# Wider r-u-k sums, one MLP step moved to an earlier slot, and weight sums spread over four slots

## The chip, the cores and the metric

The kernel runs on one core of one Trainium2 chip. The metric is the device time of one execution in microseconds (us); lower is better. TensorE does the matrix products, VectorE and GpSimd the elementwise work, ScalarE copies and activations; nearly all loads and stores go through one queue (q1 moved 54.88 of the 56.65 MB in the kernel before), issued one after another by SyncE; ScalarE issues five loads. Every timed run also has the mean clock granted to TensorE, as a share of full speed.

## The reference

Linear attention with a decay per step (RWKV-6), then a LayerNorm and an MLP with ReLU, all in fp32. Sizes: 4 batches, 8 heads, 768 steps, head width 48, model width 384, hidden width 1536.

```python
for t in range(S):
    cur = np.einsum('bhd,bhe->bhde', u[None] * kt, vt)
    y[:, :, t] = np.einsum('bhd,bhde->bhe', rt, state + cur)
    state = wt[:, :, :, None] * state + np.einsum('bhd,bhe->bhde', kt, vt)
# x: y as (B, S, 384)
xn = (x - mu) / np.sqrt(var + 1e-06) * g_ln
out = x + np.maximum(xn @ w_ch1, 0.0) @ w_ch2
```

The term with u needs, for each step and head, the sum over d of r, u and k: the "r-u-k sums".

## The kernel before

The sequence is cut into eight rounds of 384 steps (a batch and a half of the sequence each), a round into two units of four heads. Inside a round, six levels combine ever longer pieces; each level is one *slot*: TensorE forms level products (`a_ps`), VectorE multiplies r and k by decays (`rkT`) and keeps part of the products (`A`). The MLP of an earlier round is cut into steps of a few products (an h or o step is three products of 128x384, each two instructions in the profile, of 323 ns at full clock), and `fill` runs steps between the other tasks of a slot until `UNTIL[slot]` steps are done in all. So `UNTIL` says where in time the MLP's work lies. Rounds are counted from 0 and slots from the first of round 1, so slot 12 is the first of round 3.

```python
UNTIL = [3, 6, 8, 11, 14, 16, 19, 21, 24]
while len(UNTIL) <= 2 * NLEV + NLEV - 2:
    UNTIL.append(UNTIL[-1] + 3)             # slots 12 to 16: 36, 39, 42, 45, 48
while len(UNTIL) < NR * NLEV:
    UNTIL.append(UNTIL[-1] + MLP_STEPS / NLEV)
...
def fill(until, tasks):
    n = int(until + 0.01) - done
    m = max(n, len(tasks))
    for i in range(m):
        for t in tasks[i * len(tasks) // m : (i + 1) * len(tasks) // m]:
            t()
        for _ in range((i + 1) * n // m - i * n // m):
            mlp_step()
```

The r-u-k sums of the first four units are products with a selector that has two columns, one for each head of a pair:

```python
def product_sums(q):
    ...
    for pr in pairs:
        for c in range(TT):
            PE.matmul(ps[:, ts(pr * TT + c, 2)], a["ruk"][pr][:, ts(c, P)],
                      sel[:, NP * g + pr], start=True, stop=True)
```

From round 2 on the second MLP product is done with fewer multiplications (seven products in place of eight), for which VectorE forms four sums of weights once, in slots 17 to 19; the fourth is `nat_r<-more,w_sb` and `more<-more,w_sb` in the profile. `warm(n)` runs products on zeros ("idle" in the profile) that keep TensorE busy.

Of the kernel before, what the change touches and what calls it, by code (L numbers as in the profile page):

```python
# [52 lines left out]
def kernel(  # L53
# [19 lines left out]
    P = 128  # L73
    HP = 64
    C = 64
    NH = 4
    NP = NH // 2
    U = H // NH
    TT = 3
    RN = TT * P  # L80
    NHALF = S // RN
    NK = NP * TT
# [123 lines left out]
    sel = const.tile([P, H // 2, 2], F32, name="sel")  # L206
# [27 lines left out]
    for lev in range(NLEV - 1):  # L234
        n = 1 << lev
# [212 lines left out]
    def product_sums(q):  # L448
        b, f, g = units[q]
        a = st[q]  # L450
        ps = ps_t.tile([P, RN], F32, tag="t", name=f"own_ps{q}")
        for pr in pairs:
            for c in range(TT):
                PE.matmul(
                    ps[:, ts(pr * TT + c, 2)], a["ruk"][pr][:, ts(c, P)],
                    sel[:, NP * g + pr], start=True, stop=True,
                )
        o = a["own"] = p4.tile([P, TT, NH], F32, tag="own", name=f"own{q}")
        ACT.copy(
            out=o.rearrange("p c (r j) -> p r c j", j=2),  # L460
            in_=ps[:, 0 : 2 * NK].rearrange("p (r c j) -> p r c j", r=NP, j=2),
        )

    def own_term(q, eng):
# [443 lines left out]
    def mixed(*lists):  # L908
        return [
            t for _, t in sorted(  # L910
                (((i + 0.5) / len(l), t) for l in lists for i, t in enumerate(l)),
                key=lambda at: at[0],
            )
        ]

    def each(f, *ranges):
        calls = [()]
        for r_ in ranges:
            calls = [c + (x,) for c in calls for x in r_]
        return [lambda c=c: f(*c) for c in calls]  # L920
# [43 lines left out]
    for lev in range(1, NLEV):  # L964
        quads(u0, lev)
        quads(u1, lev)
        run(ahead[2 * lev - 2 : 2 * lev] if lev < NLEV - 1 else [])
        if lev in (2, 3, 4):
            begin()
        if lev == 1:  # L970
            product_sums(u0)
        elif lev < NLEV - 1:
            warm(3)
        for which in ("rk",) if lev < NLEV - 1 else "kr":
            for q in (u0, u1):
                grow(q, lev, which)
        keep(0, lev)
# [11 lines left out]
    exchanged(u0)  # L989
    states(u1)  # L990
    product_sums(u1)
    own_term(u1, POOL)
    scratch = st[u0]["rk"]
# [26 lines left out]
    UNTIL = [3, 6, 8, 11, 14, 16, 19, 21, 24]  # L1020
    while len(UNTIL) <= 2 * NLEV + NLEV - 2:
        UNTIL.append(UNTIL[-1] + 3)
    while len(UNTIL) < NR * NLEV:
        UNTIL.append(UNTIL[-1] + MLP_STEPS / NLEV)
    ahead = [t for nm in "wkr" for t in each(turned, units_of(2), nm, pairs)]
    JOINS, BEGINS = (3, 4, 4, 4, 4, 2), (3, 3, 4, 4, 3)
    for rnd in range(1, NR + 1):
# [3 lines left out]
        for lev in range(NLEV):  # L1031
            slot = (rnd - 1) * NLEV + lev
# [20 lines left out]
            tasks, turning = [], []  # L1053
            if rnd == 1:
                if lev < 2:
                    tasks += each(load, new, "kr"[lev], [SPO])
                if lev == 2:
                    SPO.dma_start(
                        out=u_bc,
                        in_=bass.AP(  # L1060
                            tensor=u.tensor, offset=u.offset, ap=[[0, P], [D, H], [1, D]]
                        ),
# [16 lines left out]
            if rnd == 2 and lev == 2:  # L1079
                tasks += each(load_before, new[:1], [k], [0], [SPO]) + each(load_v, new)  # L1080
                tasks += each(load_before, new[:1], [v], [1], [SPO])
            if slot in (17, 18, 19):
                tasks += each(weight_sums, ((3,), (1,), (2, 4))[slot - 17])
            if rnd == 2 and lev in (3, 4):
                tasks += each(own_term, now[lev - 3 :][:1], [POOL])
            if rnd > 2 and lev == 1:
# [24 lines left out]
            if lev == 3 and rnd > 1:  # L1111
                for q in now:
                    load_vx(q)
                if rnd > 2:
# [6 lines left out]
                    tasks = each(norm, [rnd - 1]) + tasks  # L1121
# [17 lines left out]
            if lev == NLEV - 1:  # L1139
# [7 lines left out]
                if now:  # L1147
                    tasks = mixed(
                        tasks,
                        each(ends, now, pairs) + each(finish, [2, 2, 4])  # L1150
                    )
                if rnd == 1:
                    tasks = [join] * JOINS[lev] + tasks + each(totals, [rnd + 1], [POOL])
            if rnd == 1 and lev < NLEV - 1:

                n = (1, 2, 2, 1, 0, 0)[lev] * NP
                tasks += mixed(
                    [begin] * BEGINS[lev], [join] * JOINS[lev], ahead[:n],
                    each(product_sums, now) if lev == 1 else [],
                )  # L1160
                del ahead[:n]
# [35 lines left out]
```

## Time and profile before

| | before |
|---|---|
| median of the first four runs | 560.83 us (559.22 to 561.71) |
| span of the profiled run | 558.1 us |
| TensorE busy | 539.5 us |
| its waits over 1 us for VectorE | 2.08 us at 167, 2.96 us at 250 |
| stretches at half clock | three, 13.6 us in all |

A table of stretches shows where time lies. I cut it into five (the second, like the last at full clock, is left out). Each line has a stretch of the span, its length, busy time and instructions of TensorE, its weight loads, VectorE, ScalarE and GpSimd, then the granted clock, the share of the DMA engines and GB/s. The cuts are at the statistics of rounds 0, 1, 2 and 3. Of the kernel before:

```profile
0.00:46.00 46.00, 43.84 (x1002) 34.81 (x1002) 32.73 (x66) 24.40 (x52) 17.72 (x54) 0.93 0.78 176
...
124.00:195.00 71.00, 66.17 (x1006) 42.54 (x1005) 59.76 (x98) 14.85 (x32) 28.07 (x22) 0.95 0.57 128
195.00:256.00 61.00, 57.35 (x922) 38.00 (x921) 50.40 (x84) 14.87 (x32) 23.60 (x18) 1.00 0.52 114
256.00:558.00 302.00, 297.52 (x3818) 221.59 (x3816) 163.22 (x335) 67.49 (x144) 60.59 (x55) 1.00 0.30 68
```

More than half of the span, from 256 us on, is TensorE back to back at full clock: 297.5 of 302 us. Nothing that only rearranges work has much to gain there. The clock is short of 1.00 in the first and third stretch, and the fourth has TensorE idle for 3.65 us, most of it the one wait at 250.

### The profile page before, as it was taken

To read this page: it belongs to the slowest core of one execution; us is meant where nothing else is said; L and a number is where in the kernel's file an instruction comes from. 1 tells how busy PE (TensorE), PEld (TensorE's weight loads), DVE (VectorE), ACT (ScalarE), POOL (GpSimd) and SP (SyncE) were. 2 spreads that over 40 slices of the span, in tenths; PEclk is the share of its full clock that TensorE was granted. 3 is DMA by queue.
4 is the path that set the end of the run, shared out by engine and by line. 5 is a ranking of instruction groups with operands and counts; after the bars stand their busy time and mean duration, and the time that the engine had idled before them with its cause. 6 is when DMAs were issued, how large, how long until landed. Compare 5 with 4: busy or idle time off the path is not lost.

```text
span 558.1 us, 18693 instructions
## 1 busy us (share of the span) xinstructions
PE 539.5 (97%) x8114; PEld 387.6 (69%) x8114; DVE 372.7 (67%) x720; ACT 169.6 (30%) x363; POOL 136.8 (25%) x157
## 2 busy tenths in 40 slices
PE   9999999999989999979999999999999999999997
PEld 6777665675656665658766895679766885688567
DVE  4888998959978777988576866778593641251022
ACT  3576887501250016201242015301331025202200
POOL 7140010300764019600482018221460000000000
PEclk9899999999997999999999999999999999999999
DMA  9956877255664584345764484547500000000001
GB/s 234 197 129 134 195 216 187 52 108 95 161 153 95 142 161 92 80 109 123 150 137 96 106 171 109 115 106 148 116 5 3 16 29 1 2 16 28 1 0 42
DMA packets 141554, 56.65 MB, mean 102 GB/s; under 512 B 124449, under 2 KB 130721, under 8 KB 141473
## 3 DMA queue, kind: packets, MB, share of 16 engines
q1 hardware_dynamic: 139600, 54.88, 43.5%
q8 instruction: 63, 1.03, 0.8%
q10 hardware_dynamic: 1872, 0.59, 0.4%
q14 instruction: 19, 0.15, 0.1%
HBM read 48.66 MB, written 4.72 MB: 96 GB/s over the span
## 4 chain that ended last, share of the span: by engine, by line
PE 70%; DVE 13%; DMA 5%; ACT 4%; SPq 3%; issue 2%; POOL 2%; DVEq 0%; ACTq 0%; POOLq 0%
PE h_ps L49 22%; PE z_ps L49 8%; PE a_ps L49 8%; PE o_ps L49 6%; PE x_ps L49 6%; PE y_ps L49 4%; PE v_ps L49 4%; PE y L49 4%; DVE rkT L49 4%; DVE w_sb L49 2%; SPq L165 2%; PE kv L49 2%; DMA r_runs<-in_r_dram 1%; DMA nat_r<-in_r_dram 1%; ACT low L49 1%
## 5 line engine op out<-in xcount | busy, mean ns | idle before, releaser
L49 PE MATMUL h_ps<-xT,w_sb 128*128 128x384 f32 x576 | 198.6, 493 | 2.6 <-ACT hs L49 1.0
L49 PEld LDWEIGHTS h_ps<-xT,w_sb 128*128 128x128 f32 x576 | 104.9, 190 | 71.0 <-ACT hs L49 4.8
L49 ACT ACTIVATE hs<-h_ps 128x384 f32<-128x384 f32 x96 | 47.0, 489 | 160.0 <-PE h_ps L49 159.2
L49 DVE TENSOR_TENSOR rkT<-rkT,tot 128x768 f32<-128x768 f32 (+1 forms) x96 | 79.7, 873 | 21.7 <-PE a_ps L49 12.3
L49 PEld LDWEIGHTS a_ps<-rkT 48*64 48x64 f32 x4128 | 66.4, 138 | 21.0 <-issue 11.6
L49 PE MATMUL a_ps<-rkT 48*64 48x32 f32 x4128 | 71.4, 222 | 3.3 <-DVE rkT L49 3.1
L49 PE MATMUL z_ps<-w_sb,hs 128*128 128x384 f32 x144 | 50.4, 495 | 3.0 <-DVE x L49 3.0
L49 PE MATMUL o_ps<-w_sb,hs 128*128 128x384 f32 x144 | 51.6, 506 | 0.1
L49 POOL TENSOR_TENSOR vo<-v,own 128x576 f32<-128x576 f32 x16 | 19.4, 1211 | 89.1 <-DVE own L49 53.0
L49 POOL TENSOR_TENSOR nat_w<-nat_w,nat_r 128x576 f32<-128x576 f32 x10 | 14.9, 1494 | 106.5 <-DMA nat_w<-in_v_dram 88.9
L49 PEld LDWEIGHTS z_ps<-w_sb,hs 128*128 128x128 f32 x144 | 26.3, 190 | 19.0 <-DVE x L49 3.1
L49 DVE SCALAR_TENSOR_TENSOR s<-s,decay,kv 128x48 f32<-128x48 f32 x160 | 29.3, 257 | 15.0 <-PE kv L49 14.9
L49 PEld LDWEIGHTS o_ps<-w_sb,hs 128*128 128x128 f32 x144 | 26.9, 195 | 17.1 <-issue 1.2
L49 DVE COPY_PREDICATED A<-mask,a_ps 128x768 f32<-128x768 int8 x32 | 38.4, 1198 | 0.0
L49 ACT ACTIVATE rstd<-mv,eps 128x3 f32<-128x3 f32 x8 | 2.4, 297 | 116.9 <-DVE mv L49 116.9
L49 DVE TENSOR_TENSOR x<-y,vo 128x288 f32<-128x288 f32 x32 | 13.1, 450 | 32.5 <-PE y L49 32.4
L49 ACT ACTIVATE xT<-xT_ps,g_sb 128x384 f32<-128x384 f32 x24 | 13.3, 580 | 41.8 <-PE xT_ps L49 41.5
L49 DVE TENSOR_TENSOR low<-hs 128x768 f32<-128x768 f32 x12 | 11.5, 962 | 21.5 <-ACT hs L49 21.5
L49 DVE TENSOR_TENSOR rkT<-rkT,wT 128x768 f32<-128x768 f32 x16 | 24.9, 1591 | 0.9 <-PE a_ps L49 0.8
L49 PE MATMUL y_ps<-w_sb,hs 128*128 128x192 f32 x144 | 25.4, 326 | 0.0
L49 PEld LDWEIGHTS y_ps<-w_sb,hs 128*128 128x128 f32 x144 | 23.4, 190 | 0.0
L49 DVE TENSOR_SCALAR w_sb<-w_sb 128x384 f32<-128x384 f32 (+1 forms) x48 | 20.5, 427 | 0.8
(120 smaller groups left out, 767.7 us busy)
## 6 DMA issues: line engine op xcount, KB each, us to landing
raw<-in_moe_w_ch_dram SPq DMA_DIRECT2D x24, 384.0 KB, 4.0
w_runs<-in_w_dram SPq DMA_DIRECT2D x79, 70.0 KB, 2.0
k_runs<-in_k_dram SPq DMA_DIRECT2D x79, 70.0 KB, 2.0
r_runs<-in_r_dram SPq DMA_DIRECT2D x79, 70.0 KB, 2.0
v<-in_v_dram SPq DMA_DIRECT2D x48, 96.0 KB, 3.3
out_dram<-x SPq DMA_DIRECT2D x24, 192.0 KB, 2.5
nat_r<-in_r_dram SPq DMA_DIRECT2D x42, 96.0 KB, 3.2
nat_k<-in_k_dram SPq DMA_DIRECT2D x42, 96.0 KB, 3.3
```

The lines of the kernel that those rows point to most:

```text
L49: return lambda *args, **kw: self.tc.keep_in_program_order(f(*args, **kw))
L165: eng.dma_start(out=t[ds(HP * j + SQ * e, SQ), 0:n], in_=bass.AP(tensor=src.tensor, offset=first + SQ * e, ap=[[NS * D, SQ], [1, n]]),)
```

## The change

The intent is to keep TensorE at full clock and to take waits from it, without changing what is computed: the r-u-k sums stream 64 columns (32 copies of the two) and ScalarE copies two of each 64; slot 12 gets four MLP steps in place of three, which is paid back in slot 16; the fourth weight sum moves from slot 19 to slot 20.

```diff
 PE.matmul(
-    ps[:, ts(pr * TT + c, 2)], a["ruk"][pr][:, ts(c, P)],
-    sel[:, NP * g + pr], start=True, stop=True,
+    ps[:, ts(pr * TT + c, HP)].rearrange("p (n j) -> p n j", j=2),
+    a["ruk"][pr][:, ts(c, P)],
+    sel[:, NP * g + pr][:, None].broadcast_to([P, HP // 2, 2]),
+    start=True, stop=True,
 )
 ...
-    in_=ps[:, 0 : 2 * NK].rearrange("p (r c j) -> p r c j", r=NP, j=2),
+    in_=ps.rearrange("p (r c n) -> p r c n", r=NP, n=HP)[..., 0:2],
 ...
+UNTIL[12:16] = [37, 40, 43, 46]
 ...
-if slot in (17, 18, 19):
-    tasks += each(weight_sums, ((3,), (1,), (2, 4))[slot - 17])
+if 17 <= slot <= 20:
+    tasks += each(weight_sums, [(3, 1, 2, 4)[slot - 17]])
```

## The prediction

> **What bounds the kernel now.** I read, in this order, the page's shares of busy time, its strip of forty slices, the clock in half-microsecond windows around each dip, the timelines of TensorE and VectorE around its long waits, and the chain of waits. First the shares and the clock strip:
>
> ```profile
> PE 539.5 (97%) x8114; PEld 387.6 (69%) x8114; DVE 372.7 (67%) x720; ACT 169.6 (30%) x363; POOL 136.8 (25%) x157
> PEclk9899999999997999999999999999999999999999
> core 0: 558.1 us, clock 0.988
> ```
>
> TensorE is busy 97% of the span, so only three things can shorten the span: fewer idle gaps on it, a higher clock, or less work. The clock strip has two weak places, slices 1 to 2 and slice 12. A mean clock of 0.988 means 0.012 x 558.1 = 6.7 us of full-speed work lost. Half-microsecond windows (busy time, instructions, granted clock, DMA share, GB/s) show three dips at half clock:
>
> ```profile
> 23.00:23.50 0.50, 0.50 (x23) 1.00 0.67 111
> 23.50:24.00 0.50, 0.50 (x5) 0.54 0.94 183
> 26.50:27.00 0.50, 0.50 (x32) 0.55 0.98 286
> 40.50:41.00 0.50, 0.50 (x7) 0.61 0.00 0
> 44.00:44.50 0.50, 0.50 (x40) 0.98 0.00 0
> 166.50:167.00 0.50, 0.00 (x0) 0.90 0.59 152
> 173.50:174.00 0.50, 0.50 (x3) 0.77 0.15 28
> ```
>
> The dips run from 23.5 to 26.9, from 40.6 to 44.0 and from 166.9 to 173.7: 3.4, 3.4 and 6.8 us, 13.6 in all, half of which is the 6.8 lost. Next, TensorE's timeline (start, length) just ahead of the dips and at its only other long wait:
>
> ```profile
> 20.25 1.50 PE L49 MATMUL own_ps<-sel,ruk 128*128 128x2 f32 x12 [0.24 <-ACT wT L49]
> 37.82 1.50 PE L49 MATMUL own_ps<-sel,ruk 128*128 128x2 f32 x12
> 164.24 0.92 PE L49 MATMUL kv<-v,kn 64*64 64x48 f32 x48
> 167.24 1.51 PE L49 MATMUL a_ps<-rkT 48*64 48x32 f32 x48 [2.08 <-DVE rkT L49]
> 169.29 1.50 PE L49 MATMUL a_ps<-rkT 48*64 48x32 f32 x48 [0.54 <-DVE rkT L49]
> 250.24 2.20 PE L49 MATMUL z_ps<-w_sb,hs 128*128 128x384 f32 x6 [2.96 <-DVE x L49]
> ```
>
> Both early dips follow a window holding the r-u-k sums (two columns streamed per weight load). The third follows a TensorE wait of 2.08 us for VectorE. The last line is a 2.96 us wait without a dip. VectorE's timeline ahead of that one:
>
> ```profile
> 234.70 2.05 DVE L49 TENSOR_TENSOR nat_r<-more,w_sb 128x768 f32<-128x768 f32 x1
> 236.68 0.55 DVE L49 TENSOR_TENSOR more<-more,w_sb 128x384 f32<-128x384 f32 x1
> 237.15 2.90 DVE L49 STREAM_TRANSPOSE wT<-w_runs 128x384 f32<-128x384 f32 x4
> 248.29 0.84 DVE L49 STREAM_TRANSPOSE rkT<-r_runs 128x384 f32<-128x384 f32 x1 [1.17 <-DMA r_runs<-in_r_dram]
> 249.85 0.34 DVE L49 TENSOR_TENSOR x<-z_ps,x 128x192 f32<-128x192 f32 x1
> ```
>
> The x add that TensorE waits for stands in VectorE's order behind a transpose that waits for a load of r. In the chain of waits that load was issued late because the k and r loads reuse the buffers that the four wT transposes free, and those stand behind the fourth weight sum (the first two lines).
>
> [...]the three dips lie on one grid of 3.41 us. [...]12 r-u-k instructions of the chain at 66.98 us take 1.24, or 103 ns each, although only two columns stream. [...]the sum of 128x768 took 2.05 us at 234.70 beside GpSimd, the like one at 210.84 took 0.94.
>
> **Part one: 64 columns in the r-u-k sums.** Four calls of six products, each two instructions. A 128x384 instruction takes 1.94/6 = 323 ns, so 64 columns need an estimated 54 ns of streaming, under the 103 ns of the weight load: the six products keep their 1.24 us. Transposes, with 128 columns, take 1.46/12 = 122 ns, so at worst each call grows 0.1 us. The ScalarE copy still moves 12 values per partition. So the direct cost is 0 to 0.3 us in all. What it buys is activity: 12 x 54 = 0.65 us more streaming in a window of 3.41. Counting for each window streaming time weighted by the share of rows used (columns x 0.84 ns), I get 0.38 and 0.57 for the windows before the first two dips. They become 0.57 and 0.76. Windows that did not trip lie at 0.54 and above; but one of the tripped ones was at 0.57, so the measure is crude and the first window is near the edge.
>
> If the dips go: in the first, the r transposes 1.20 against 0.81 for like ones, two filler instructions 1.28 against 0.65, level products 2.08 against 1.53: 1.6 us. In the second, filler 1.58 against 0.65 and about 100 y products that would take half of 1.9: 1.8 us. Both lie on the chain (TensorE to 45.3, then VectorE's statistics that begin the VectorE-bound stretch of weight conversion), and later waits on loads there are on buffers freed by the same engines. Full value 3.4; I count 75%: 2.5 us.
>
> **Part two: a fourth MLP step in round 3's first slot.** No work is added: the order of the built kernel has one o step of three products (2.03 us at full clock) between the last h step and the second kv of that slot, and one fewer before the last level products of round 3. In the trace's clock: h ends at 164.24, the o step runs to 166.3, kv to 167.1, the level products find their first operand ready at 167.24. Of 2.62 us of wait about 0.14 + 1.25 stay, because the second VectorE product still ends at 169.25. Then three o steps from 170.05 at full clock end at 176.1 instead of 178.26. VectorE itself does not move before 178.3: it is back to back from 162.5. Its wT transposes at 175.3 also anchor the load queue, busy issuing from 176.2 to 202, so r lands at 187.7 as before. But VectorE had 1.61 + 1.30 + 0.36 us idle after 178 and 0.71 + 2.22 later. Walking both queues on, the fourth level products start at 194.4 instead of 196.75, the sixth at 202.0 instead of 205.84, and VectorE's r-u-k reduction at 205.7 instead of 208.92. From there GpSimd and the loads follow VectorE, so 3.2 us is kept. If the dip at 166.9 stays for one window (I give it one in three), 1.6 of that goes. Counted: 2.7 us.
>
> **Part three: weight sums over four slots.** The fourth sum leaves its place ahead of the wT transposes (2.05 + 0.55[...]) for one behind the next mask copy. So the transposes, the loads and r's landing come 2.5 us earlier than part two alone makes them. VectorE then does the sum, 1.45 us, where it waited 0.41 + 0.93 + 1.17. Walking the queue: last transpose ends 243.8, x add 244.9, TensorE resumes at 245.0; it stopped at 244.1. Of the 2.96 wait 0.9 is left: 2.0 us. After 262 TensorE idles little over 1 us in total, so what is gained there reaches the end.
>
> **Sum.** 2.5 + 2.7 + 2.0 = 7.2, less 0.4 for the wider products and small new waits: 6.8. From 560.3 this gives 553.5 us.
>
> **Rivals.** (a) The clock does not answer to columns: part one yields nothing, 556. For it speaks that the windows also hold small y, kv and level products; against it, that windows full of those without r-u-k sums kept full clock. (b) The load queue takes the place of the wait: it issues without pause from 176 to 202, so parts of 3.2 us are given back there and the reduction moves by one only; 556 to 557. Against it stand the 3.6 us that VectorE waited for TensorE at 202.4. (c) [...]an earlier stretch shifts a poor window elsewhere[...]: a new dip costs 1.7; 555. (d) All goes well, no dip left: 560.3 - 3.4 - 3.2 - 2.0 = 551.7.
>
> **Range and chances.** The worst mixtures of (a), (b) and (c) give 558, the best 551; run to run the kernel before spreads 2.5 us[...]. So 549.8 to 557.8 eight times in ten. Faster by over 2% needs 549.1, below the best sum: 0.07. Slower by over 2% would need a new stall of 18 us, of which nothing speaks: 0.01. Within 2%: 0.92.
>
> **What would show it.** Right: no half clock near 24 and 41 us; r-u-k groups still about 1.24 us; the level products of round 3's second slot waiting about 1.3 instead of 2.6; o steps after them at 323 ns; the z wait near 245 under 1.2; the fourth weight sum standing between a mask copy and the transposes of k, each of them not waiting over 1 us for its load; a mean clock of 0.995 or more. Wrong: dips at the same places (rival a), long new VectorE waits on r loads near 187 to 205 (b), a dip after 167 (c).

## The result, and the profile after

The changed kernel takes 553.89 us in the median of four runs (552.47 to 555.32), against 560.83 before. The ratio is 0.988, with a 95% interval of 0.9843 to 0.9916. A ratio here is the mean time of one kernel's fast runs over that of the other's in the same rounds, so it is not quite the ratio of the medians. It is clear of 1.

First the shares, the clock strip and the mean clock of the profiled run after the change:

```profile
PE 535.8 (97%) x8114; PEld 384.7 (70%) x8114; DVE 371.4 (67%) x720; ACT 169.6 (31%) x363; POOL 137.2 (25%) x157
PEclk9999999999998999999999999999999999999999
core 0: 551.7 us, clock 0.997
```

TensorE's instructions are as many as before; one weak slice is left in the strip. The first, third and fourth of the same five stretches, cut at the same statistics:

```profile
0.00:44.00 44.00, 40.99 (x1003) 32.83 (x1004) 33.23 (x67) 24.73 (x53) 18.04 (x54) 1.00 0.78 179
...
121.00:192.00 71.00, 67.13 (x1012) 42.80 (x1012) 60.06 (x99) 14.96 (x32) 28.10 (x22) 0.98 0.55 130
192.00:250.00 58.00, 56.25 (x919) 37.52 (x918) 49.07 (x85) 14.86 (x32) 23.68 (x18) 1.00 0.52 121
```

The cuts are rounded; the statistics themselves start at 46.24, 123.69, 194.78 and 256.02 before, and at 43.82, 121.10, 192.09 and 249.63 after. So the first stretch gave 2.4 us, the second and third 0.3 together, the fourth 3.7; the last 302 us did not change. VectorE's statistics of round 1 and its r-u-k reduction, on which the reading of part two rests, before (first two lines) and after:

```profile
123.69 1.46 DVE L49 BATCH_NORM_STATS2 stats<-x 128x6 f32<-128x384 f32 x3
208.92 0.74 DVE L49 TENSOR_REDUCE own<-rk 128x12 f32<-128x576 f32 x1
121.10 1.45 DVE L49 BATCH_NORM_STATS2 stats<-x 128x6 f32<-128x384 f32 x3
204.52 0.74 DVE L49 TENSOR_REDUCE own<-rk 128x12 f32<-128x576 f32 x1
```

Now the places that the prediction named. TensorE's timeline after the change (start, length, what, wait before it):

```profile
20.13 1.55 PE L49 MATMUL own_ps<-sel,ruk 128*128 128x64 f32 x12 [0.24 <-ACT wT L49]
31.83 1.60 PE L49 MATMUL a_ps<-rkT 48*64 48x32 f32 x96 [0.73 <-DVE A L49]
...
161.27 2.10 PE L49 MATMUL o_ps<-w_sb,hs 128*128 128x384 f32 x6
163.29 0.92 PE L49 MATMUL kv<-v,kn 64*64 64x48 f32 x48
165.01 0.90 PE L49 MATMUL a_ps<-rkT 48*64 48x32 f32 x48 [0.80 <-DVE rkT L49]
167.06 1.39 PE L49 MATMUL a_ps<-rkT 48*64 48x32 f32 x48 [1.15 <-DVE rkT L49]
...
243.85 2.20 PE L49 MATMUL z_ps<-w_sb,hs 128*128 128x384 f32 x6 [1.05 <-DVE x L49]
```

The group of sums takes 1.55 us in this line, 1.50 before. The o step stands where TensorE used to wait, and of 2.62 us of wait 1.95 is left, in two gaps. The z wait is 1.05 instead of 2.96. And there is a small new wait, 0.73 us at 31.8, for VectorE. The granted clock in half-microsecond windows (busy, instructions, clock, DMA share, GB/s):

```profile
23.50:24.00 0.50, 0.50 (x6) 1.00 1.03 207
40.50:41.00 0.50, 0.50 (x45) 1.00 0.00 0
...
167.00:167.50 0.50, 0.44 (x22) 0.75 0.70 137
170.50:171.00 0.50, 0.50 (x3) 0.84 0.91 163
```

Both early dips are gone; the third is still there, behind two gaps of 0.80 and 1.15 us, one window (3.4 us) long instead of two. Finally VectorE ahead of the z wait:

```profile
237.27 0.95 DVE L49 TENSOR_TENSOR nat_r<-more,w_sb 128x768 f32<-128x768 f32 x1
238.14 0.55 DVE L49 TENSOR_TENSOR more<-more,w_sb 128x384 f32<-128x384 f32 x1
241.88 0.86 DVE L49 STREAM_TRANSPOSE rkT<-r_runs 128x384 f32<-128x384 f32 x1 [1.06 <-DMA r_runs<-in_r_dram]
243.46 0.33 DVE L49 TENSOR_TENSOR x<-z_ps,x 128x192 f32<-128x192 f32 x1
```

The fourth sum now takes 0.95 instead of 2.05 us, with no GpSimd instruction beside it (before, one ran there from 233.53 to 235.93), and it stands where VectorE waited for loads. One load wait of 1.06 us remains.

### The profile page after: what moved, and what is told of

Same layout as the page of the kernel before. It is cut to its first block, busy times and chain, and to the rows that moved or that the text cites.

```text
span 551.7 us, 18694 instructions
## 1 busy us (share of the span) xinstructions
PE 535.8 (97%) x8114; PEld 384.7 (70%) x8114; DVE 371.4 (67%) x720; ACT 169.6 (31%) x363; POOL 137.2 (25%) x157
## 4 chain that ended last, share of the span: by engine, by line
PE 71%; DVE 10%; ACT 5%; SPq 4%; DMA 4%; POOL 3%; issue 3%; DVEq 0%; POOLq 0%; ACTq 0%
PE h_ps L49 22%; PE a_ps L49 8%; PE z_ps L49 8%; PE o_ps L49 6%; PE x_ps L49 6%; PE y_ps L49 4%; PE v_ps L49 4%; PE y L49 4%; DVE rkT L49 3%; SPq L165 3%; DVE w_sb L49 2%; ACT low L49 2%; PE kv L49 1%; PE idle L49 1%; DVE A L49 1%
## 5 line engine op out<-in xcount | busy, mean ns | idle before, releaser
L49 DVE TENSOR_TENSOR rkT<-rkT,tot 128x768 f32<-128x768 f32 (+1 forms) x96 | 79.9, 875 | 22.7 <-PE a_ps L49 11.9
```

The source lines that it names most:

```text
L49: return lambda *args, **kw: self.tc.keep_in_program_order(f(*args, **kw))
```

## The experiments

Theory: each part gains by what the prediction says, and whether a dip follows a window of 3.41 us depends on how much of it the array streams columns. The second half is a guess of mine, from where the dips of the kernel before lie. Rivals: the early dips went by chance; the load queue or VectorE takes back what TensorE gains; or the clock is all that changed. Twelve kernels ran, all with five rounds, all with correct results. A batch shares its runs of the kernel before.

The dips of one profile lie on one grid. In the profile before they begin at 23.54, 40.61 and 166.90 us, 5 and 37 steps of 3.413 us apart; in that of h2_no_cols below at 22.67, 121.66 and 169.44, 29 and 14 steps apart. They lasted one, two or three steps: 3.4 us (changed kernel, from 167.25), 6.8 (before, from 166.90) and 10.2 (e2_step, from 21.83, through windows that streamed 0.79 and 0.80 by the measure below). Counted from the start of the span the grid lies elsewhere in each profile: its first line is at 3.06 us before, at 0.01 after, at 1.82 in e1_cols64 and at 2.19 in h2_no_cols. The texts below call this its phase.

### One part at a time

```diff
 e1_cols64: the kernel before with the hunks in product_sums alone
 e2_step:   the kernel before with  + UNTIL[12:16] = [37, 40, 43, 46]
 e3_sums:   the kernel before with  + tasks += each(weight_sums, [(3, 1, 2, 4)[slot - 17]])
```

> Part one alone: the r-u-k sums of the kernel before with 64 columns, nothing else. My theory ([...]the wider sums lift the two early windows from about 0.4 to about 0.6): no half clock near 24 and 41 us, the dip near 167 still there at 6.8 us, mean clock about 0.994; about 2.3 us faster than before (ratio 0.996), which is what the changed kernel shows at 43 us. Rival (the early dips went by chance of the window grid's phase, the columns do nothing): dips at 24 and 41 as before, ratio 1.000.

> Part two alone: the fourth MLP step in slot 12. My theory (the step fills idle time; the rest follows because VectorE and the load queue had slack after 178 us): early dips as before, level products of round 3's second slot wait about 2 us in two gaps, and everything from VectorE's r-u-k reduction near 209 us on comes 2.2 us earlier; the z wait stays near 3 us; ratio 0.996. Rival (the gain comes only from a shorter half clock after 167): the gain is then the clock's, at most 1.7, and goes with the dip. Rival two (the load queue, issuing without pause from 176 to 202, gives it back): ratio 0.999 or above.

> Part three alone: the fourth weight sum behind the wT transposes. My theory: the loads of k and r before the z wait are issued about 2 us earlier, the z wait falls from 3.0 to about 1.0 us, nothing else moves, 2.0 us faster, ratio 0.9965. Rival (the wait only moves to the products that use the fourth sum, or to VectorE's next level): z wait short but a new TensorE wait of 1 us or more between 250 and 265, ratio 0.999.

| run | median us | ratio to before, 95% interval | mean us below before |
|---|---|---|---|
| e1_cols64 | 560.19 | 0.9972 (0.994 to 1.0004) | 1.4 |
| e2_step | 558.59 | 0.995 (0.9921 to 0.9979) | 2.9 |
| e3_sums | 559.86 | 0.9966 (0.9934 to 0.9998) | 2.0 |

The last column is the difference of the mean times, the kernel before at 561.75 in this batch. The three add up to 6.4 us, about what the whole change gives, so no part needs another. Each interval is 0.3% to either side, as wide as an effect, and that of e1 reaches over 1; the profiles must tell the mechanism.

In e1 the early dips are gone, as expected, but the profile shows a dip that the kernel before did not have in its own, right behind the z wait (windows as above):

```profile
250.50:251.00 0.50, 0.34 (x1) 0.97 0.18 40
254.00:254.50 0.50, 0.50 (x3) 0.62 0.60 139
```

So the z wait, which no dip followed in the profile before, has one behind it here. The grids differ: before, the wait (247.28 to 250.24 us) lies across a line of the grid at 248.80, and TensorE is busy for 1.90 and 1.97 us of the 3.41 on either side; in e1 the wait (248.44 to 250.66) lies within the one window ahead of the dip (247.56 to 250.97), of which 1.19 us are left busy. That this made the difference is my reading of two profiles. With this dip the mean clock of e1's profiled run is 0.991, not the 0.994 expected.

In e2, where the clock still dips after 172 us, the two level products of slot 13 wait 1.48 and 1.15 us:

```profile
169.69 0.90 PE L49 MATMUL a_ps<-rkT 48*64 48x32 f32 x48 [1.48 <-DVE rkT L49]
171.73 1.31 PE L49 MATMUL a_ps<-rkT 48*64 48x32 f32 x48 [1.15 <-DVE rkT L49]
```

That is 2.6 us where I had expected about 2. Two more expectations were misses: the z wait fell to 1.7 us instead of staying near 3, and the r-u-k reduction stood at 209.17 us, no earlier than before (208.92), behind a single early dip of 10.2 us. The load queue did not give the step back: its rival asked for a ratio of 0.999 or above. Whether the gain is more than the clock's, these times do not show, because e2's mean clock loss (span times one minus the clock) was 7.3 us against 9.4 for the kernel before in this batch; I come back to it with the fillers. In e3, the wait summary (total, times, longest) has the z wait at 1.1 us, as expected:

```profile
PE z_ps L49 <- DVE x L49: 1.1, 1, 1.1
```

The wait of slot 13, untouched by this part, was 3.5 us in the same profile against 2.1 before: how long it is differs from run to run.

### What the clock answers to: 8, 32 and no added columns

```diff
 e4_cols8 (on before) and h32_cols (on the changed kernel):
-    .broadcast_to([P, HP // 2, 2])      # 64 columns
+    .broadcast_to([P, 4, 2])            # 8 columns
+    .broadcast_to([P, 16, 2])           # 32 columns
 h2_no_cols: the changed kernel with product_sums as before (2 columns)
```

> Part one with 8 columns in place of 64. Streaming adds only 12 x 5 ns = 0.06 us to a window of 3.41, so on my theory the windows stay at about 0.41 to 0.43, where every such window tripped: at least one early dip stays, most likely both; ratio 0.998 to 1.000. Rival (what matters is the form of the product, a strided destination or more than one column, not the streaming time): both dips gone as with 64, ratio 0.996.

> The changed kernel without part one (two-column sums). My theory: the early windows are poor for 65% and 34% of the phases, so the mean clock falls to 0.991 to 0.997 and differs from run to run, and the kernel is 2 us slower than the changed one: ratio to before 0.990 to 0.992. Rival (columns do nothing for the time, VectorE takes back what the clock gives): same as the changed kernel, 0.987.

> The changed kernel with 32 columns in place of 64 in the r-u-k sums. Streaming in the poorest early window was 0.34 with two columns, 0.36 and 0.32 with eight, 0.51 with 64. The model[...] gives 0.34 + 0.09 = 0.43, just over the 0.42 that has parted windows with a dip ahead from those without. So: no early dip in the profile, clock 0.994 to 1.000 as the changed kernel, ratio 0.988. If the limit is really higher, near 0.5, early dips stay in some runs: clock 0.991 to 0.994, ratio 0.991.

The time of e4 was 559.78 us, ratio 0.997 (0.9936 to 1.0004): not told apart from e1, so my expectation for its time is a miss. Its clock was spread, 0.982 to 0.994 in six runs, while five of e1's six runs lie at 0.991. h2 took 556.6, ratio 0.9919 (0.9882 to 0.9957), with a clock of 0.984 to 0.994 where I had expected 0.991 to 0.997; the changed kernel in the same batch (r_after, below) took 555.1, ratio 0.989. The mean times, 556.4 and 554.96, put part one at 1.4 us, the same as e1, but six runs of each spread too much to tell 1.4 us from nothing; the mean clock loss is 6.0 us against 2.3. h32 took 554.39, ratio 0.9894 (0.9868 to 0.9919).

The profiles say more. From each trace I worked out which share of a sliding window of 3.41 us the array streams: an instruction counts about 0.84 ns a column (323 ns measured for 384 columns; the tables were worked out with 1% less), twice that at half clock (two idle instructions took 1.28 us in the dip at 23.5 us, 0.65 at 28.7), overlaps once. The poorest window near each place, and the dips in that profile:

| run | 15-28 us | 31-45 us | 160-176 us | 230-256 us | dips start at |
|---|---|---|---|---|---|
| before | 0.34 | 0.34 | 0.29 | 0.08 | 23.5, 40.6, 166.9 |
| e4, 8 columns | 0.36 | 0.32 | 0.02 | 0.25 | 22.9, 166.3 |
| h2, 2 columns | 0.36 | 0.36 | 0.17 | 0.61 | 22.7, 121.7, 169.4 |
| h32, 32 columns | 0.42 | 0.52 | 0.17 | 0.67 | 23.1, 169.9 |
| e1, 64 columns | 0.51 | 0.49 | 0.16 | 0.23 | 169.0, 251.0 |
| after, 64 columns | 0.51 | 0.50 | 0.26 | 0.57 | 167.3 |

Eight profiles in all have 64-column sums (these two and six told below or in the next part): none has a dip in the first 100 us. All five with two or eight columns have one or two. That settles the first rival: the early dips did not go by chance. h32 is a miss of mine. I had added twelve instructions of 32 columns, an estimated 0.32 us or 0.09 of a window, to the 0.34 of two columns; but the window that preceded its dip, at 19.7 to 23.1 us, streamed 0.46, where I had put the limit at 0.42:

```profile
23.00:23.50 0.50, 0.50 (x25) 0.59 0.84 147
26.00:26.50 0.50, 0.50 (x17) 0.50 1.13 133
```

Ahead of the dips I found 0.17 to 0.46, and windows of 0.38 (e3, from 61.6 us) to 0.49 that no dip followed; so the statement in an expectation below, that 0.42 parted them all, was too strong. Between 0.38 and 0.46 both kinds occur, so my measure does not part them. Two dips do not fit it at all: those at 121.7 us in h2 and at 122.2 in the run with fillers followed windows that streamed 0.59, nearly all of it level products, whose form in the profile is 48*64 where that of the MLP's products is 128*128. A count that weights each product by its form (48*64 over 128*128 is 0.19) and adds products whose records overlap takes them in: it gives these two windows 0.25 and 0.28, and all 22 windows ahead of a dip 0.33 or less, but 12 windows of 0.25 to 0.33 had no dip behind them. It was fitted afterwards, and no run was made to test it; what the chip answers to is not shown.

### Is it the clock alone? Fillers in place of moved work

```diff
 g1_fillers: e1_cols64, and after states/outputs of slot 13 and of slot 21
+if slot == 13:
+    warm(9, "t")
+if slot == 21:
+    warm(9, "t")
```

> The changed kernel again, as the yardstick for this batch and for more runs of its clock. Sliding a 3.41 us window over the profiles so far, the array streamed less than 0.42 of the window ahead of every dip and more than that ahead of every window without one. On the profile of the changed kernel only round 3's second slot still has such windows, for 46% of the grid's phases. So: mean clock 1.000 in about half of the runs and 0.997 or a little lower in the others, ratio 0.985 to 0.990.

> Part one, and in place of parts two and three idle products (three of 128x384 on zeros, 1.94 us) in TensorE's two long waits, in slot 13 ahead of the level products and in slot 21 ahead of the z products. No work is moved, so only the clock can gain. My theory (parts two and three gain by moved work and earlier loads, and by the clock besides): clock 0.997 to 1.000, but the waits are only occupied, not shortened: 2 to 3 us faster than before, ratio 0.995, and 4 us slower than the changed kernel. Rival (the clock is all that the change gained): ratio 0.987 as the changed kernel.

g1 took 557.5 us, ratio 0.9929 (0.9889 to 0.997), mean 557.2; the changed kernel in the same batch 555.1 (552.35 to 556.81), ratio 0.989 (0.9851 to 0.9928), mean 554.96, before 561.13. The clock of g1 (0.993 to 1.000, mean loss 1.7 us) is at least as good as the changed kernel's (0.994 to 0.997, mean loss 2.3), and in the mean it is still 2.2 us slower. That points to moved work for the rest of the gain but does not show it: the two intervals overlap, and 0.5 of the 2.2 us lies outside the core's span (g1's times exceed their spans by 1.7 to 2.7 us, the changed kernel's by 1.7). Against the 4 us expected, the difference is a miss by half.

The profiles say more for the moved step. Parts one and three touch nothing between the statistics of round 1 and the r-u-k reduction. With two windows of half clock in it, this stretch took 85.2, 85.7, 85.7 and 87.4 us without the step (before, e4, g1, e1) and 83.8 with it (h2); in g1 and h2 the first of the two began up to 1.0 us ahead of it. With the step, it took 83.4 to 84.7 with one such window (after, r_after, h32, e2) and 82.7 and 82.8 with none (f3, r_after2). So the step gains 1.5 us or more at an equal count of dips, though only one profile stands on its side, and a window of half clock costs 0.6 to 2.0.

r_after was as expected in time; none of its six runs was at 1.000, where I had expected half.

### A step more, and fillers in the gaps

```diff
 f1_fifth: the changed kernel with
-UNTIL[12:16] = [37, 40, 43, 46]
+UNTIL[12:16] = [38, 41, 44, 47]
 f2_both: f1_fifth and
+UNTIL[18:20] = [UNTIL[18] + 1, UNTIL[19] + 1]
 f3_gaps: the changed kernel, ahead of each unit's level products
+if slot == 13:
+    warm(3, "t")
```

> The changed kernel with a fifth MLP step in slot 12 and the steps up to slot 15 one further. My theory: the 0.8 and 1.15 us gaps before the level products of slot 13 are filled, no window under 0.42 is left anywhere, clock 1.000 in nearly every run; one step less remains before round 3's sixth level, so VectorE's r-u-k reduction comes up to 2 us earlier: 551 to 552 us, ratio to before 0.982. Rival (VectorE and the load queue already set that stretch, so a further step buys the clock only): ratio 0.986, that is at most 0.5 us better than the changed kernel.

> The fifth step in slot 12 as in the run with five, and one step more in slots 18 and 19 counted cumulatively (one less in slot 20). In the run with five, TensorE waited 0.43 and 1.15 us for VectorE near 218 us, and 39% of the phases have a poor window there. My theory (a gap that the earlier step uncovers can be filled the same way): those waits under 0.5 us in sum or no dip after them, clock 0.999 to 1.000, about 2 us faster than with five: 551.5 to 552.5, ratio to before 0.982 to 0.984. Rival (loads and GpSimd set VectorE's pace from 176 to 217, so TensorE being earlier buys nothing but the clock): within 0.7 us of the run with five, ratio 0.9865.

> The changed kernel once more, so that the two others are compared with it on the same chip: ratio to before 0.987 to 0.990, clock 0.994 to 1.000, and the profile with at most one dip, after 167 us.

> The changed kernel with one idle product of 128x384 (two instructions, 0.65 us) ahead of each unit's level products in slot 13, that is in each of the two gaps that the fourth step left (0.80 and 1.15 us). The poorest window there streamed 0.17 to 0.27; two fillers add 1.3 of 3.41 us, so 0.55. My theory (the last dip goes, nothing waits for the fillers): no dip in the profile, clock 0.999 to 1.000 in nearly every run, and a time as the fastest runs of the changed kernel, 552.4 to 553, ratio to before 0.985 to 0.987. Rival (VectorE, not the clock, sets the pace after 167 us, so that a dip there costs nothing): clock 1.000 but time as before the fillers, near 554, ratio 0.988.

| run | median us (range) | ratio, 95% interval | clocks |
|---|---|---|---|
| f1_fifth | 553.82 (552.98 to 555.14) | 0.9871 (0.9838 to 0.9903) | 0.994 to 1.000 |
| r_after, same batch | 555.1 (552.35 to 556.81) | 0.989 (0.9851 to 0.9928) | 0.994 to 0.997 |
| f2_both | 553.08 (551.0 to 557.97) | 0.9887 (0.9849 to 0.9926) | 0.991 to 1.000 |
| r_after2, same batch | 552.85 (552.38 to 553.13) | 0.9871 (0.9843 to 0.9899) | 1.000, once 0.996 |
| f3_gaps | 553.45 (552.4 to 554.28) | 0.9877 (0.9836 to 0.9919) | 1.000, once 0.997 |

None is clear of the changed kernel, and the times that I had expected (551 to 552 us for f1, 551.5 to 552.5 for f2, 552.4 to 553 for f3) were missed in the median by all three. In f1 the gaps of slot 13 are filled and the dip there is gone, but a wait of the same form appears one round on, with a dip of two windows behind it. TensorE in f1, and VectorE ahead of it:

```profile
218.73 0.90 PE L49 MATMUL a_ps<-rkT 48*64 48x32 f32 x48 [0.43 <-DVE rkT L49]
220.78 1.47 PE L49 MATMUL a_ps<-rkT 48*64 48x32 f32 x48 [1.15 <-DVE rkT L49]
```

```profile
205.04 0.75 DVE L49 TENSOR_REDUCE next<-nat_w 128x12 f32<-128x576 f32 x1 [2.26 <-POOL nat_w L49]
```

VectorE now waits 2.26 us for GpSimd, which had itself waited for the load of `nat_w` until 203.5 us. That is the load queue of rival (b): with the fourth step it had room (in the changed kernel GpSimd was done with `nat_w` at 202.8, and VectorE came to it at 205.2), with a fifth it sets the pace. f2 fills the gaps at 218 and has its wait and dip later still:

```profile
241.36 3.89 PE L49 MATMUL z_ps<-w_sb,hs 128*128 128x384 f32 x6 [1.88 <-DVE x L49]
```

f3 shows the fillers in the gaps, and no dip in the whole profile:

```profile
165.59 0.91 PE L49 MATMUL idle<-nought 128*128 128x384 f32 x2
166.44 0.90 PE L49 MATMUL a_ps<-rkT 48*64 48x32 f32 x48
167.27 0.91 PE L49 MATMUL idle<-nought 128*128 128x384 f32 x2
```

Its median lies between r_after and r_after2, and five of its six runs have a clock of 1.000. Its ratio, 0.9877, is nearer to the rival's 0.988 than to mine; the stretches above still show what a dip there costs. The sixth, at 0.997, has no profile. A version that beats the changed kernel beyond noise was not found.

### How much a dip costs

Across the 44 timed runs of the kernel before in the four batches, the mean clock went from 0.979 to 0.994, with the program the same. The 15 runs that lost under 7.3 us to the clock took 559.1 us in the mean, the 19 that lost over 9.5 took 562.6: 3.5 us of time for 4.5 us of clock. So roughly three quarters of what the clock loses is seen in the time; that the rest is hidden in waits that are there anyway is my reading, not shown. The mean loss was 8.5 us before and 1.7 us in the 14 runs of the changed kernel. As an estimate from these numbers, three quarters of the 6.8 us between them, some 5 us of the 6.9 by which the mean times differ (560.9 and 554.0), are the clock's.

## Why the prediction was right

The predicted time was 553.5 us and the measured 553.89, inside the range; the chances put "within 2%" first. That it came within 0.4 us is luck: the changed kernel's medians in three batches were 553.89, 555.1 and 552.85. The terms below come from the two profiles of the change; the profiles of the other runs move the term of each part by half a microsecond or more. Step by step:

- *Part one, 2.5 us counted as 75% of 3.4.* Both dips went and the sums cost 0.05 us a group, within the 0.1 allowed for (in the chain of waits the later two groups went from 1.23 and 1.24 to 1.28 and 1.29); the activity argument held (eight profiles against five). The first statistics came 2.4 us earlier. But the 2.4 owe something to which profiles were drawn: over all runs these statistics began at 43.8 to 45.4 us with 64 columns (eight profiles, mean 44.6) and at 45.3 to 47.2 with two or eight (five, mean 46.3), 1.7 us apart. In time, the single part measured 1.4 us both ways (e1, h2), below the 2.5. Why less than the full 3.4 came is argued, not shown: not that a dip stayed, but that VectorE may have taken part back, of which the 0.73 us wait at 31.8 is one piece. The working's crude measure does not come out either: it puts all windows without a dip at 0.54 and above, but by its own count the window from 61.1 us stood at 0.41 without a dip.
- *Part two, 2.7 us.* The walk through the queues gave 1.39 us of wait left; 1.95 was left, and the dip that I gave one chance in three to stay did stay in the profile, for one window; over 14 runs, 10 had a clock under 1. VectorE's r-u-k reduction moved from 208.92 to 204.52, 4.4 us; less the 2.6 brought along from the second statistics (123.69 to 121.10), that is 1.8. In the two profiles that is the term that was mis-sized, and part of the 1.8 is the dip, one window shorter than before; e2 alone measured 2.9 in time. Over all runs the stretch from the second statistics to the reduction took 86.3 us in the mean of the five profiles without the step and 83.6 in the seven with the fourth, 2.7 apart, dips included.
- *Part three, 2.0 us.* From that reduction to the end of the z wait it was 41.32 us before and 39.33 after: 2.0. The wait fell to 1.05 where 0.9 was worked out, and the sum by itself took 1.50 where 1.45 was. e3 alone measured 2.0. Here too the profile before was the long one: the same stretch took 40.0 to 41.3 us in the four profiles without this part (before, e1, e4, e2; mean 40.6) and 39.0 to 39.5 in six with it (mean 39.2), 1.4 apart. The working puts the fourth sum, 2.05 + 0.55 us beside GpSimd, at 1.45 without it, because the like sum at 210.84 took 0.94 us. That GpSimd made the difference is not shown: the like sum also had a GpSimd instruction beside it, from 211.01; there it was that one which took longer, 1.79 us (the same one 1.15 at 215.13 in f1).
- *Sum.* 2.4 + 0.2 (from the first to the second statistics) + 1.8 + 2.0 = 6.4, the difference of the two profiled spans, against 6.8 predicted.

The 103 ns of a weight load in the prediction need a word: they are a rate. The twelve r-u-k instructions of a group came one in 103 ns by the chain of waits (1.24 us), and their loads one in 112 by their own records (twelve in 1.42 us, the last 0.19 long); the single records of these loads last 186 to 192 ns and overlap.

What the prediction did not see is that a dip is not a property of a place. It read three dips off one profile, and took the z wait for a place without one. The kernel before loses 8.5 us to the clock in the mean, where its profile showed 6.8, and in e1, with that wait unchanged in the program, a dip did follow it, at 250.97 us. Part three, which shortens the wait, may therefore also remove a dip in some runs, to which the prediction gave no value. Rival (a) fell with the 64-column profiles, rival (b) did not bind here but did with the fifth step, and the gaps in slot 13, behind which rival (c) has its dip after 167, are what f3 fills.

## What to carry to other kernels

Where TensorE's clock dips, look at how much of the time ahead of the dip the array streams, not only at how much of it the profile calls busy: here TensorE was busy for 3.29 of the 3.41 us ahead of the dip at 23.54, but the poorest window near it streamed 0.34, and no profile with 64-column sums (0.51) had that dip. Padding these thin products from two columns to 64 cost 0.05 us a group, and idle products in two gaps no time that could be measured. A dip seen in one profile, or missed in it, need not be so in the next run: over 44 runs of one program the mean clock went from 0.979 to 0.994. So look at the clock of many runs before giving a dip a value. A moved step pays only until the next engine or queue sets the pace: here the fourth step did pay (e2_step, 2.9 us in the mean), and no gain of the fifth could be measured (f1_fifth, a ratio of 0.9871 against 0.989).
